# Joint layer norms: the mean subtracted in the application, epsilon added on GpSimd

## The chip, the cores and the metric

The kernel runs on one NeuronCore of a Trainium2 chip. A core has five engines that run side by side, each through its own list of instructions in order: TensorE (PE, matmuls into PSUM), VectorE (DVE), ScalarE (ACT), GpSimd (POOL) and SyncE (SP, which here only issues transfers). They wait for one another by semaphores. The metric is the device time of one execution in microseconds (us). Before the change three runs took 243.38, 243.4 and 242.79 us, the median 243.38.

## The reference

One transformer block over x of 2048 rows by 512. A vector c gives six rows of 512 (sa, ca, ga, sb, cb, gb) that scale and shift. The first half is attention with a sliding window: 32 heads of width 16, each query seeing the 256 last keys. The second half mixes over rows ("token MLP"): two products with w1 (2048 x 1792) and w2 (1792 x 2048) along the row axis. There are three layer norms: of x ahead of the attention, of the sum behind it, and a third at the start of the mixer.

```python
def _layernorm(x, axis=-1, eps=1e-05):
    m = jnp.mean(x, axis=axis, keepdims=True)
    v = jnp.var(x, axis=axis, keepdims=True)
    return (x - m) / jnp.sqrt(v + eps)
...
h = _layernorm(x, axis=-1) * (1 + ca) + sa
x = x + ga * _A_ref(h, A_wqkv, A_wo)          # attention
h = _layernorm(x, axis=-1) * (1 + cb) + sb
x = x + gb * _B_ref(h, B_w1, B_b1, B_w2, B_b2)  # third norm of h, then u = gelu(h^T w1 + b1), y = u w2 + b2
```

## The kernel before

**Tiling.** x lies in 16 blocks of 128 rows (`xres`, named x). Four blocks make a group. Per group the first norm gives xn, which TensorE transposes to h1T (L1142, evacuated by VectorE at L1155 with the scale and shift on the way). From h1T come K, Q and V by matmuls with wqkv (L606 in whole columns, L610 in four column tiles; both are the helper `dense_step`), which VectorE or ScalarE copy out of PSUM (L740, L738: KT, QR, V). Q is padded to QP with a parity mask (L1048). Score matmuls (L819, L837, L847) with mask matmuls (L828, L859) fill a PSUM tile pss of 128 x 1024, of which there are three; ScalarE turns each into et by one exponential (L868), 152 in all. TensorE multiplies et by V (L890) into one of two single banks bk; VectorE transposes the product (t, L899), takes reciprocals (zr, L908), GpSimd merges (L912), VectorE transposes again (OT, L921). The output product with Wo is added to x (L1255).

**Norms.** A norm of one block runs: statistics and their aggregation on VectorE (L599, L600), giving mean and variance in mv; `prepare`, two steps on VectorE, variance plus epsilon (ve, L571) and minus the mean (ng, L575); `rstd`, two steps on GpSimd, ve to the power -1/2 (r, L582) and ng times r (sh, L584); and per block `apply`, x times r plus sh (L592 on VectorE or GpSimd, L588 on ScalarE). Blocks may be normed jointly: their statistics lie side by side, and the four steps between are done once for two or four blocks. The first norms of groups 1 to 3 (n1) are joint over four blocks. Behind the attention, n2 and n3 are joint over 4, 2, 4, 1 and 4, 2, 2, 1 blocks in groups 0 to 3, so the last group norms each block for itself. That makes twelve joint norms (three n1, four n2, five n3) and eight single ones. The first group's own norm, in the opening, has code of its own: the helper `rstd_of` (L553, L555) adds epsilon and takes the power on GpSimd, and L683 subtracts the mean and multiplies on VectorE.

**Second half.** h is scaled by a row (bc_cb) and shifted by a row (bc_sb) at L1273, normed again to hb, and the mixer's first product runs over hb with w1 (L606), in part during the attention, to fill TensorE between the scores. Behind the attention TensorE does what is left of it, ScalarE the gelu, and then the second product with w2 (L1451), whose results VectorE finishes (L1460, L1464) for the store.

**What sets the order.** Everything between the opening and the second product is a task with an engine, an estimated cost, dependencies, a rank from the table `PLACES`, and an engine choice from the table `BY`. The planner `Order` simulates the engines with these costs, picks task after task, and the instructions are emitted in that order; on the chip each engine keeps it. The two steps of `prepare` are one task (`e1`, `e2`, `e3`) of 0.13 us on VectorE, and `rstd` one (`r1`, `q2`, `q3`) on GpSimd. Tiles come from pools that turn over; the small ones (mv, ve, ng, r, sh) four deep for each name.

Of the kernel before, what the change touches and what calls it, by code (L numbers as in the profile page):

```python
# [10 lines left out]
ALU = mybir.AluOpType  # L11
# [336 lines left out]
def kernel(  # L348
# [202 lines left out]
    def rstd_of(var, n, name):  # L551
        ve = small.tile([P, n], DT.float32, name=name + "_ve")
        nc.gpsimd.tensor_scalar(out=ve[:], in0=var, scalar1=EPS, scalar2=0.0, op0=ALU.add, op1=ALU.add)  # L553
        r = small.tile([P, n], DT.float32, name=name)
        nc.gpsimd.tensor_tensor(out=r[:], in0=ve[:], in1=mhalf[:, 0:n], op=ALU.pow)  # L555
        return r

    class Norm:
# [8 lines left out]

        def prepare(self):
            n = self.n
            self.ve = small.tile([P, n], DT.float32, name=self.name + "ve")  # L570
            nc.vector.tensor_scalar(  # L571
                out=self.ve[:], in0=self.mv[:, :, 1], scalar1=EPS, scalar2=0.0, op0=ALU.add, op1=ALU.add
            )
            self.neg = small.tile([P, n], DT.float32, name=self.name + "ng")
            nc.vector.tensor_scalar(  # L575
                out=self.neg[:], in0=self.mv[:, :, 0], scalar1=-1.0, scalar2=0.0, op0=ALU.mult, op1=ALU.add
            )

        def rstd(self):
            n = self.n  # L580
            self.r = small.tile([P, n], DT.float32, name=self.name + "r")
            nc.gpsimd.tensor_tensor(out=self.r[:], in0=self.ve[:], in1=mhalf[:, 0:n], op=ALU.pow)  # L582
            self.shift = small.tile([P, n], DT.float32, name=self.name + "sh")
            nc.gpsimd.tensor_tensor(out=self.shift[:], in0=self.neg[:], in1=self.r[:], op=ALU.mult)  # L584

        def apply(self, eng, i, out, src):
            if eng == "ACT":
                nc.scalar.activation(  # L588
                    out=out, in_=src, func=ACT.Identity, bias=self.shift[:, i : i + 1], scale=self.r[:, i : i + 1]
                )  # L590
            else:
                (nc.vector if eng == "DVE" else nc.gpsimd).tensor_scalar(  # L592
                    out=out, in0=src, scalar1=self.r[:, i : i + 1], scalar2=self.shift[:, i : i + 1],
                    op0=ALU.mult, op1=ALU.add,
                )
# [906 lines left out]
```

## Time and profile before

| | |
|---|---|
| median of three runs | 243.38 us |
| the profiled execution | 242.64 us, of which its span 240.9 us |
| busy: TensorE, VectorE, ScalarE, GpSimd | 234.5, 177.3, 162.1, 96.1 us |
| granted TensorE clock | 1.00 throughout |
| instructions of VectorE, GpSimd | 421, 149 |

How to read it: a row of a timeline has the start in us from the span's start, the duration in us, engine, line, operation and the tiles it writes and reads (output <- inputs), how many neighbours were merged, and in brackets the engine's idle time before it with the instruction that ended that. [...] A row of the waits has who waited for whom, the sum in us, how many times, and the longest. A row of stretches has from and to, the length, and then busy us of each engine with its instructions in brackets, the clock, the share of the DMA engines and GB/s; of one line alone, only the engines that have it.

### The profile page before, as it was taken

Reading aid. Unit: us, or ns where it says so; the run is one execution under the profiler, and the core shown is the slowest. Engines: PE = TensorE matmul, PEld = TensorE weight load, DVE = VectorE, ACT = ScalarE, POOL = GpSimd, SP = SyncE. Lnnn points to the kernel's source line nnn. Section 1 sums busy time; section 2 is a strip of 40 time slices with the busy share of each in tenths; the row PEclk is TensorE's granted clock in tenths of the full one; section 3 lists DMA queues with packets and bytes.
Section 4 is the critical chain, followed back from the end, with each engine's and each line's share of the span. In section 5 each row is a group of like instructions: output and inputs, shape, how many; then the busy total and the mean of one; then the engine's idle time right before and its main releaser. Section 6 shows DMA issues by size and latency. Waiting matters only on the chain.

```text
span 240.9 us, 9884 instructions
## 1 busy us (share of the span) xinstructions
PE 234.5 (97%) x4358; PEld 118.7 (49%) x4358; DVE 177.3 (74%) x421; ACT 162.1 (67%) x188; POOL 96.1 (40%) x149
## 2 busy tenths in 40 slices
PE   7999999999999999999999999999999999999994
PEld 2545555545655554554454455454444444444443
DVE  8799998878999899999356867989964306060644
ACT  7589999999999999999999999900446400000000
POOL 5319775741655466996310113686920000000000
PEclk9999999999999999999999999999999999999999
DMA  5998714063160343210110110069999001111031
GB/s 161 303 345 245 224 32 123 21 169 68 58 181 5 74 113 91 64 35 7 33 38 14 26 38 3 3 199 393 413 405 407 18 0 46 44 44 44 24 111 44
DMA packets 26151, 28.09 MB, mean 117 GB/s; under 512 B 10488, under 2 KB 23292, under 8 KB 26108
## 3 DMA queue, kind: packets, MB, share of 16 engines
q1 hardware_dynamic: 25956, 27.33, 36.0%
q8 instruction: 34, 0.56, 1.0%
q10 hardware_dynamic: 152, 0.13, 0.2%
q14 instruction: 9, 0.07, 0.1%
HBM read 22.55 MB, written 2.10 MB: 102 GB/s over the span
## 4 chain that ended last, share of the span: by engine, by line
PE 74%; DVE 19%; POOL 2%; issue 2%; ACT 2%; DVEq 0%; ACTq 0%; POOLq 0%
PE bk L606 18%; PE pss L1451 15%; PE bk L890 7%; PE pss L606 6%; PE bk L610 6%; PE pss L847 6%; DVE stats L599 5%; PE bk L1451 5%; PE bk L624 3%; DVE x L1255 2%; DVE t L899 2%; PE pss L859 2%; PE pss L819 2%; PE pss L828 1%; DVE QR L740 1%
## 5 line engine op out<-in xcount | busy, mean ns | idle before, releaser
L868 ACT ACTIVATE et<-pss 128x1024 bf16<-128x1024 f32 x152 | 141.7, 1050 | 1.5 <-PE pss L859 1.3
L1451 PEld LDWEIGHTS <-w2r 128*128 128x128 bf16 x238 | 23.1, 98 | 25.5
L912 POOL TENSOR_TENSOR merge<-t,zr 128x512 bf16<-128x512 f32 x16 | 16.9, 1058 | 32.3 <-DVE zr L908 32.2
L1460 DVE SCALAR_TENSOR_TENSOR o<-pss,bFM,bc_gb 128x512 bf16<-128x512 f32 (+2 forms) x13 | 8.8, 705 | 27.9 <-PE pss L1451 27.9
L1451 PE MATMUL pss<-guT,w2r 128*128 128x512 bf16 (+2 forms) x130 | 28.4, 363 | 0.0
L899 DVE STREAM_TRANSPOSE t<-bk 128x512 f32<-128x512 f32 x32 | 22.6, 706 | 7.2 <-PE bk L890 7.0
L847 PE MATMUL pss<-QP,KT 32*128 32x64 bf16 (+2 forms) x672 | 24.2, 236 | 0.7 <-DVE QP L727 0.3
L606 PE MATMUL bk<-h1T,wqkv 128*128 128x512 bf16 x80 | 21.0, 381 | 0.0
L1048 POOL TENSOR_SCALAR QP<-QR,mask_par 128x512 bf16<-128x512 bf16 x22 | 15.1, 694 | 14.8 <-PE pss L859 9.7
L606 PE MATMUL bk<-hb,w1a 128*128 128x512 bf16 x82 | 20.6, 380 | 0.2 <-DVE t L899 0.2
L606 PE MATMUL pss<-hb,w1b 128*128 128x512 bf16 x80 | 20.1, 379 | 0.1
L847 PEld LDWEIGHTS <-KT 32*128 32x128 bf16 x672 | 11.2, 92 | 17.7 <-issue 15.1
L890 PE MATMUL bk<-et,V 128*32 128x256 bf16 (+2 forms) x704 | 19.0, 240 | 0.7 <-DVE t L899 0.4
L599 DVE BATCH_NORM_STATS2 stats<-x 128x6 f32<-128x512 bf16 x28 | 18.8, 673 | 0.2
L890 PEld LDWEIGHTS <-V 128*32 128x32 bf16 x704 | 15.2, 97 | 7.2 <-issue 2.7
L606 PEld LDWEIGHTS <-w1b 128*128 128x128 bf16 x112 | 10.9, 98 | 13.7 <-issue 0.5
L859 PE MATMUL pss<-mask_q,mask_k 32*128 32x256 bf16 x240 | 17.5, 268 | 0.0
L606 PE MATMUL bk<-wod,OT 128*128 128x512 bf16 x54 | 13.9, 381 | 0.0
L606 PEld LDWEIGHTS <-w1a 128*128 128x128 bf16 x90 | 7.9, 98 | 10.3 <-issue 2.5
L606 PE MATMUL bk<-wqkv,h1T 128*128 128x512 bf16 x47 | 12.8, 381 | 0.0
L1255 DVE TENSOR_TENSOR x<-bk,x 128x512 bf16<-128x512 f32 x16 | 10.8, 674 | 2.8 <-PE bk L606 2.8
L921 DVE STREAM_TRANSPOSE OT<-merge 128x512 bf16<-128x512 bf16 x16 | 11.2, 700 | 2.0 <-POOL merge L912 1.8
(145 smaller groups left out, 396.5 us busy)
## 6 DMA issues: line engine op xcount, KB each, us to landing
w2r<-in_B_w_dram SPq DMA_DIRECT2D x14, 512.0 KB, 10.6
w1a<-in_B_w_dram SPq DMA_DIRECT2D x16, 224.0 KB, 3.7
w1b<-in_B_w_dram SPq DMA_DIRECT2D x8, 448.0 KB, 6.7
wmod<-in_w_mod_dram SPq DMA_DIRECT2D x4, 512.0 KB, 6.9
x<-in_A_x_dram SPq DMA_DIRECT2D x15, 128.0 KB, 5.4
out_dram<-otile SPq DMA_DIRECT2D x15, 128.0 KB, 1.8
VL<-V SPq DMA_DIRECT2D x15, 96.0 KB, 2.3
wmod<-in_w_mod_dram SPq DMA_DIRECT2D x4, 256.0 KB, 4.3
```

Of the source, the lines that this page charges most:

```text
L599: nc.vector.bn_stats(out=stats[:], in_=src)
L606: nc.tensor.matmul(out[:], lhsT=lhsT, rhs=rhs, start=start, stop=stop, skip_group_check=True)
L610: nc.tensor.matmul(out[cols, :], lhsT=lhsT[:, cols], rhs=rhs, start=start, stop=stop, tile_position=(0, 32 * j), skip_group_check=True,)
L847: mm(pss[j // 2][:, j % 2, c0 : c0 + nq], lhsT=keys(4 * tg + kb)[rows[j], :], rhs=QP[s][rows[j], par, q0 : q0 + nq], start=n == 0, stop=False,
L859: mm(o, lhsT=mask_k[rows[j], 0:P], rhs=rhs, start=False, stop=True, tile_position=(32 * j, 0), skip_group_check=True,)
L868: nc.scalar.activation(out=et[:], in_=held.pop(("pss", u, a))[:], func=ACT.Exp, scale=SCORE_SCALE)
L890: nc.tensor.matmul(po[32 * j : 32 * j + 32, q0 : q0 + nq], lhsT=v(j), rhs=held["et", s, k, j // 2][:, j % 2, c0 : c0 + nq], start=n == 0, ...
L899: nc.vector.transpose(out=held["t2", s][:, par, :], in_=psum.pop(("po", s, par))[:])
L912: nc.gpsimd.tensor_tensor(out=m[:].rearrange("p (b a d) -> p a b d", a=2, d=DH), in0=t2v(s, 0, DH, DH), in1=held["zr", s][:].to_broadcast( ...
L1048: engine[by(f"Qp{s}.{par}", "POOL")].tensor_scalar(out=QP[s][:, par, :], in0=QR[s][:], scalar1=mask_par[:, par : par + 1], scalar2=0.0, op ...
L1255: nc.vector.tensor_tensor(out=xres[tb][:], in0=pa[:], in1=xres[tb][:], op=ALU.add)
L1451: nc.tensor.matmul(py[:, lo:hi], lhsT=w2r[:, fc, tb * P : (tb + 1) * P], rhs=guT[fc][:, lo:hi], start=fc == made[0], stop=fc == made[-1], ...
```

## The change

For a norm of more than one block, `prepare` emits nothing. `rstd` calls `rstd_of`, so GpSimd adds epsilon to the variance itself and then takes the power; the product of mean and r is not formed. `apply` subtracts the mean and multiplies by r, where it multiplied by r and added a shift. Single norms are as before; they alone are applied on ScalarE, which needs the shift.

```diff
         def prepare(self):
             n = self.n
+            if n > 1:
+                return
             self.ve = small.tile([P, n], DT.float32, name=self.name + "ve")
...
         def rstd(self):
             n = self.n
+            if n > 1:
+                self.r = rstd_of(self.mv[:, :, 1], n, self.name + "r")
+                return
             self.r = small.tile([P, n], DT.float32, name=self.name + "r")
...
+            elif self.n > 1:
+                (nc.vector if eng == "DVE" else nc.gpsimd).tensor_scalar(
+                    out=out, in0=src, scalar1=self.mv[:, i, 0:1], scalar2=self.r[:, i : i + 1],
+                    op0=ALU.subtract, op1=ALU.mult,
+                )
             else:
```

The helper it calls is there already:

```python
    def rstd_of(var, n, name):
        ve = small.tile([P, n], DT.float32, name=name + "_ve")
        nc.gpsimd.tensor_scalar(out=ve[:], in0=var, scalar1=EPS, scalar2=0.0, op0=ALU.add, op1=ALU.add)
        r = small.tile([P, n], DT.float32, name=name)
        nc.gpsimd.tensor_tensor(out=r[:], in0=ve[:], in1=mhalf[:, 0:n], op=ALU.pow)
        return r
```

The planner's costs are not touched, so its order of tasks is the same. The lists of TensorE, ScalarE and SyncE are unchanged; VectorE's has 24 instructions fewer, GpSimd's as many as before. In the changed kernel line numbers from the diff on are higher by up to 10. In the rows below the number behind a tile's name tells buffers apart, and brackets name whom an instruction waits for.

VectorE, before, where the transposes of the second group are evacuated to h1T (28 us in the profile):

```order
L740 CAST QR<-bk_846 128x512 [waits PE_49]
L1155 TENSOR_SCALAR h1T<-bk_862,modFM_93 128x512 [waits PE_49]
L1155 TENSOR_SCALAR h1T<-bk_862,modFM_93 128x512
L571 TENSOR_SCALAR n1ve<-n1mv 128x4 [waits DVE_49]
L575 TENSOR_SCALAR n1ng<-n1mv 128x4
L1155 TENSOR_SCALAR h1T<-bk_900,modFM_94 128x512 [waits PE_49]
L1155 TENSOR_SCALAR h1T<-bk_900,modFM_94 128x512
```

VectorE, after, at the same place:

```order
L750 CAST QR<-bk_842 128x512 [waits PE_49]
L1165 TENSOR_SCALAR h1T<-bk_858,modFM_93 128x512 [waits PE_49]
L1165 TENSOR_SCALAR h1T<-bk_858,modFM_93 128x512
L1165 TENSOR_SCALAR h1T<-bk_896,modFM_94 128x512 [waits PE_49]
L1165 TENSOR_SCALAR h1T<-bk_896,modFM_94 128x512
```

The two pairs of evacuations, which had the third group's two small steps between them, now follow each other.

GpSimd, before, from the application of block 5's second norm on (103 us in the profile):

```order
L592 TENSOR_SCALAR h_3663<-x_69,n2r,n2sh 128x512
L582 TENSOR_TENSOR n3r<-n3ve,mhalf 128x2 [waits DVE_49]
L584 TENSOR_TENSOR n3sh<-n3ng,n3r 128x2 [waits DVE_49,Pool_49]
L1273 TENSOR_TENSOR h_3663<-h_3663,bc_cb_99 128x512
L592 TENSOR_SCALAR hb_116<-h_3408,n3r,n3sh 128x512 [waits Pool_49]
L1273 TENSOR_TENSOR h_3663<-h_3663,bc_sb 128x512 [waits Pool_49]
```

GpSimd, after, at the same place:

```order
L597 TENSOR_SCALAR h_3635<-x_69,n2mv,n2r 128x512
L553 TENSOR_SCALAR n3r_ve<-n3mv 128x2 [waits DVE_49]
L555 TENSOR_TENSOR n3r<-n3r_ve,mhalf 128x2 [waits Pool_49]
L1283 TENSOR_TENSOR h_3635<-h_3635,bc_cb_99 128x512
L597 TENSOR_SCALAR hb_116<-h_3384,n3mv,n3r 128x512 [waits Pool_49]
L1283 TENSOR_TENSOR h_3635<-h_3635,bc_sb 128x512 [waits Pool_49]
```

The addition of epsilon now stands ahead of the power, where the product stood behind it; the wait for VectorE is now for the statistics themselves, and everything else keeps its place.

VectorE, before, where those results are taken up (108 us):

```order
L599 BN_STATS stats<-h_3663 128x6 [waits Pool_49]
L600 BN_AGGR n3mv<-stats 128x2 [waits DVE_49]
L571 TENSOR_SCALAR n3ve<-n3mv 128x2 [waits DVE_49]
L575 TENSOR_SCALAR n3ng<-n3mv 128x2
L899 STREAM_TRANSPOSE t_3884<-bk_3787 128x512 [waits PE_49,Pool_49]
L592 TENSOR_SCALAR hb_117<-h_3399,n3r,n3sh 128x512
```

VectorE, after:

```order
L609 BN_STATS stats<-h_3635 128x6 [waits Pool_49]
L610 BN_AGGR n3mv<-stats 128x2 [waits DVE_49]
L909 STREAM_TRANSPOSE t_3848<-bk_3755 128x512 [waits PE_49,Pool_49]
L597 TENSOR_SCALAR hb_117<-h_3375,n3mv,n3r 128x512
```

The transpose t, which frees a bank for TensorE, now follows the aggregation directly.

## The prediction

> **What bounds the kernel now.** I read the page's busy shares first, then the stretches, then the waits of TensorE, then the timelines of single engines. The page and the table of stretches (us, then busy time of PE, PEld, DVE, ACT, POOL) say:
>
> ```profile
> PE 234.5 (97%) x4358; PEld 118.7 (49%) x4358; DVE 177.3 (74%) x421; ACT 162.1 (67%) x188; POOL 96.1 (40%) x149
> ...
> 13.00:33.00 20.00, 19.34 (x432) 10.16 (x429) 19.58 (x48) 19.55 (x24) 12.83 (x19) 1.00 0.75 232
> 33.00:110.00 77.00, 76.41 (x2124) 41.00 (x2124) 71.12 (x153) 76.93 (x85) 47.89 (x59) 1.00 0.31 80
> 110.00:123.00 13.00, 12.75 (x374) 6.71 (x374) 7.73 (x16) 12.96 (x15) 4.35 (x7) 1.00 0.10 20
> 123.00:157.00 34.00, 33.84 (x904) 17.63 (x906) 26.15 (x57) 33.49 (x36) 9.88 (x12) 1.00 0.10 21
> 157.00:190.00 33.00, 32.94 (x208) 14.99 (x197) 24.19 (x66) 10.40 (x15) 15.29 (x28) 1.00 0.87 334
> ```
>
> From 13 to 157 us two engines are full at once, TensorE with matmuls and ScalarE with the exponentials; from 157 on it is TensorE alone. The chip is not throttled (the clock column is 1.00). VectorE, whose 24 small steps go, is nearly full too up to 110 us, but a VectorE step is worth time only where TensorE or ScalarE waits for it. The waits of TensorE say where:
>
> ```profile
> PE bk L890 <- DVE t L899: 0.4, 1, 0.4
> PE bk L610 <- DVE h1T L1155: 0.3, 1, 0.3
> ...
> PEld L819 <- ACT et L868: 2.5, 6, 0.4
> ```
>
> The last row is ScalarE's hold on TensorE (a score matmul waits until an exponential has emptied its PSUM). It returns all through the attention, so a TensorE gain is given back at the next such wait unless ScalarE moves too. ScalarE's own rhythm:
>
> ```profile
> 25.86 5.77 ACT L868 ACTIVATE et<-pss 128x1024 bf16<-128x1024 f32 x6
> ...
> 32.03 68.60 ACT L868 ACTIVATE et<-pss 128x1024 bf16<-128x1024 f32 x74 [0.40 <-PE pss L859]
> ...
> 110.58 6.90 ACT L868 ACTIVATE et<-pss 128x1024 bf16<-128x1024 f32 x7
> ...
> 32.03 1.02 ACT L868 ACTIVATE et<-pss 128x1024 bf16<-128x1024 f32 x1 [0.40 <-PE pss L859]
> ```
>
> One takes 1.02, and 74 in a row start (68.60 - 1.02) / 73 = 0.926 apart. Twice the rhythm breaks. The sixth of the first row starts at 25.86 + 5.77 - 1.02 = 30.61, the next at 32.03: 1.42 apart, 0.50 lost. From 110.58 seven stand (6.90 - 1.02) / 6 = 0.98 apart: 6 x 0.054 = 0.32 lost. These are the two places that the change can reach, since each lies right behind one of the two TensorE waits on VectorE above.
>
> **The change, part by part.** Removed: in the twelve joint norms, all before 162 us, the additions of epsilon (L571) and the negations of the mean (L575) on VectorE.
>
> ```profile
> 0.00:162.00 162.00, 2.98 (x12) 1.00 0.36 98
> ...
> 0.00:162.00 162.00, 2.79 (x12) 1.00 0.36 98
> ```
>
> That is 2.98 + 2.79 = 5.77 us of VectorE in 24 instructions. Where no long GpSimd instruction is in the way a pair costs 0.14 from start to start (below, 109.34 to 109.48); four steps took far longer, and three of them stand in the chain that ended last. If every piece counted, this would be the gain; two places count.
>
> First place, the evacuation of the second group's transposes; the second row of GpSimd is what n1ng meets:
>
> ```profile
> 27.43 0.98 DVE L1155 TENSOR_SCALAR h1T<-bk,modFM 128x512 bf16<-128x512 bf16 x2
> 28.34 0.16 DVE L571 TENSOR_SCALAR n1ve<-n1mv 128x4 f32<-128x4 f32 x1
> 28.41 0.60 DVE L575 TENSOR_SCALAR n1ng<-n1mv 128x4 f32<-128x4 f32 x1
> 28.91 0.98 DVE L1155 TENSOR_SCALAR h1T<-bk,modFM 128x512 bf16<-128x512 bf16 x2
> ...
> 27.62 1.36 POOL L1048 TENSOR_SCALAR QP<-QR,mask_par 128x512 bf16<-128x512 bf16 x2 [0.46 <-DVE QR L740]
> ...
> 29.95 1.05 PE L610 MATMUL bk<-wqkv,h1T 128*32 128x512 bf16 x16 [0.35 <-DVE h1T L1155]
> ```
>
> n1ng ends at 29.01, when GpSimd's QP pair does (28.98): it stood still behind QP. Without the two steps the second pair of h1T starts 0.57 earlier (28.34 for 28.91). TensorE's 0.35 is then covered, and VectorE's earlier removed pair (0.14, same group of work, VectorE full) can add to it, so the matmuls come 0.35 to 0.49 earlier, and with them the mask matmul for which ScalarE sat idle at 32.03. ScalarE could take up to 0.50. I take 0.45. ScalarE keeps its rhythm behind that, so the gain reaches 110 us.
>
> Second place, the evacuation that TensorE awaits at 110.25, with GpSimd's work ahead of it:
>
> ```profile
> 98.63 0.87 POOL L582 TENSOR_TENSOR n2r<-n2ve,mhalf 128x2 f32<-128x2 f32 x1 [0.35 <-DVE n2ng L575]
> ...
> 103.42 0.77 POOL L592 TENSOR_SCALAR h<-x,n2r,n2sh 128x512 bf16<-128x512 bf16 x1
> 104.29 0.81 POOL L582 TENSOR_TENSOR n3r<-n3ve,mhalf 128x2 f32<-128x2 f32 x1
> 105.18 0.20 POOL L584 TENSOR_TENSOR n3sh<-n3ng,n3r 128x2 f32<-128x2 f32 x1
> ...
> 107.20 1.16 POOL L1273 TENSOR_TENSOR h<-h,bc_sb 128x512 bf16<-128x512 bf16 x1
> ...
> 108.39 0.69 DVE L599 BATCH_NORM_STATS2 stats<-h 128x6 f32<-128x512 bf16 x1 [0.15 <-POOL h L1273]
> ...
> 109.34 0.17 DVE L571 TENSOR_SCALAR n3ve<-n3mv 128x2 f32<-128x2 f32 x1
> ...
> 109.48 0.71 DVE L899 STREAM_TRANSPOSE t<-bk 128x512 f32<-128x512 f32 x1
> ...
> 110.25 0.63 PE L890 MATMUL bk<-et,V 128*32 128x256 bf16 x24 [0.35 <-DVE t L899]
> ```
>
> VectorE's own part: ve and ng right ahead of the transpose, 0.14. The other 0.21 of TensorE's 0.35 must come from GpSimd, since the statistics at 108.39 wait for its addition at 107.20, and whatever VectorE saves before that ends in this wait.
>
> Added on GpSimd: an addition of epsilon in each joint norm, where the product n..sh (L584) goes.
>
> ```profile
> L553 POOL TENSOR_SCALAR r_ve<-mv x2: 242/270/298, 4.9 to 6.7; 128x2 f32<-128x2 f32 x2
> ```
>
> 0.20 goes (105.18 above), 0.27 comes by the same line in the kernel's opening (0.24 to 0.30, for two blocks; I take it for four as well): 12 x 0.07 = 0.84 us more on GpSimd in all, hidden wherever GpSimd waits anyway. At 98.28 it sits idle for 0.35 until n2ng is done; the addition needs only the mean and variance, so it lies in that idle time, the power starts at 98.63 as before, and 0.28 (product and its gap of 0.08) is gained. At 104.19 GpSimd is busy up to then: addition and gap 0.35, product and gap 0.28 less, and the 0.10 before the power gone: 0.03 gained. Together 0.31, more than the 0.21 needed. So this wait goes too; ScalarE's 0.32 is the price. The bounds are 0.12 (ve and ng alone) and 0.32; I take 0.32. Behind 110 TensorE meets ScalarE again, as two score groups of the same form show, the second stretched by such a wait; so nothing above 0.32 passes. The last row is the wait at 151.6, behind both places:
>
> ```profile
> 112.89 0.43 PE L819 MATMUL pss<-QP,KT 32*64 32x128 bf16 x32
> ...
> 122.00 0.55 PE L819 MATMUL pss<-QP,KT 32*64 32x128 bf16 x32
> ...
> 151.63 0.59 PE L606 MATMUL bk<-hb,w1a 128*128 128x512 bf16 x2 [0.16 <-DVE t L899]
> ```
>
> The application changes its operations, not its count: 13 on VectorE, 23 on GpSimd.
>
> ```profile
> 0.00:162.00 162.00, 5.06 (x13) 16.96 (x23) 1.00 0.36 98
> ...
> L683 DVE TENSOR_SCALAR xn<-x,mv,r x4: 378/399/800, 6.5 to 8.5; 128x512 bf16<-128x512 bf16 x4
> ```
>
> On VectorE subtract and multiply is what L683 does already: 0.40 against 5.06 / 13 = 0.39, cost nothing. On GpSimd no row shows that pair of operations; it now takes 16.96 / 23 = 0.74. The low bound is QP's 0.68 (1.36 / 2), the high one the 1.16 of a two-tensor instruction; I take 0.74, as the form and the bytes stay. What the mean must wait for is no later than before, since the statistics precede r. The buffers of mean and variance are held up to the last application instead of the second step; they turn over four deep, and the fifth norm of a kind comes long after the first one's last application, so no wait comes of it. No DMA is touched, and no row of TensorE, ScalarE or SyncE.
>
> In the 33 us behind 157 TensorE has 32.94 of work, so the joint norm that is still open there has nobody waiting. The transpose awaited at 151.6 is the end of a run of VectorE work without a removed step in it, and that wait stays. The sum is 0.45 + 0.32 = 0.77, about 0.8 us. Against the profiled execution (242.64, its span 240.9 and 1.7 around it) that gives 241.8. The median of the three runs, 243.38, lies 0.74 above the profiled one, and the forecast against it is 243.38 - 0.8 = 242.6.
>
> **The rivals.** *The stall is handed on.* QP kept GpSimd busy up to 28.98 and a VectorE step behind it; if the next VectorE instruction stood still as long, nothing would be gained there, and likewise at 103.7: 243.3. Against it speaks that the first pair of h1T ran its 0.98 from 27.43 under the same QP, exactly as the second pair did later. [...]
>
> *Only the first place pays.* If the addition costs GpSimd more than the idle time covers, 0.45 + 0.12 remain: 242.8.
>
> *The whole chain pays.* The chain that ended last runs through VectorE for long, and holds
>
> ```profile
> 28.50 0.51 DVE n1ng L575
> ...
> 86.64 0.70 DVE n3ve L571
> ...
> 103.73 0.48 DVE n3ve L571
> ```
>
> 1.7 us in three steps: 241.7. Against it: TensorE had 76.41 of 77 us busy between 33 and 110, so 1 us is not there to be had; the chain shows one path, not how near the next is.
>
> *Slower: GpSimd's subtract and multiply costs like two-tensor work.* Five applications lie between 96.7 and 108.4:
>
> ```profile
> 96.70:108.40 11.70, 0.00 (x0) 3.84 (x5) 1.00 0.15 40
> ```
>
> At 1.16 each, 0.39 more than 3.84 / 5 = 0.77, the addition at 107.20 comes 2.0 later, less 0.3; TensorE at 110.25 waits 1.7 more, and ScalarE starves behind it. With 0.45 kept that is 1.2 slower: 244.6. It decides from (0.45 + 0.3) / 5 = 0.15 us per application on. For it: nothing in the trace prices that pair on GpSimd. Against it: VectorE takes the same time for both pairs, and the bytes moved are the same.
>
> **How the numbers follow.** 0.3% of 243.38 is 0.73 us, about what a measurement of this kernel can tell from no change. Forecast 0.62, with a range of its own from 242.2 to 243.0; its centre lies just past the bound, and as the early 0.14 and ScalarE's 0.50 lie above what I took, I put two thirds of it (0.41) beyond. The whole chain 0.09; first place only 0.10; handed on 0.06; slower 0.12, and 0.01 for what I don't see. Faster 0.41 + 0.09 = 0.50, same 0.21 + 0.10 + 0.06 = 0.37, slower 0.13. The range 241.7 to 243.6 leaves out the slower case and half of the whole-chain one, 0.17.
>
> **What would show it.** In the changed kernel's profile VectorE has 24 instructions fewer and some 5.5 us less busy time; the wait of L610 on h1T near 29.5 is gone and ScalarE's idle 0.40 near 31.5 is under 0.1; the wait of L890 on t near 109.5 is gone, and seven exponentials there take 6.6; GpSimd's application stays at 0.74 and its new addition at 0.27. An application above 0.9, or a TensorE wait on GpSimd or VectorE of over 0.5 anywhere between 30 and 157 us, would make the forecast wrong; so would ScalarE as slow as now with the two waits gone.

## The result, and the profile after

The changed kernel takes 261.86 us (median of six runs, 260.81 to 263.41) beside 242.83 us for the kernel before in the same comparison: a ratio of 1.0783, 95% interval 1.0740 to 1.0826. It is 19 us slower; 242.6 was forecast. The profiled execution's span is 258.7 us, 17.8 more than before.

The page of the changed kernel, busy times and the granted clock in 40 slices:

```profile
PE 234.2 (91%) x4316; PEld 120.1 (46%) x4358; DVE 174.9 (68%) x397; ACT 162.6 (63%) x188; POOL 126.7 (49%) x149
...
PEclk9999997999999999959999999999999999999999
```

TensorE and ScalarE are busy as long as before (the trace lacks the records of 42 matmuls), VectorE 2.4 us less, in 24 instructions fewer. GpSimd has 30.6 us more in the same 149 instructions. The answer on the application's line L597 (count, then ns least/median/most, first and last start) has all of it:

```profile
L597 POOL TENSOR_SCALAR hb<-h,n3mv,n3r x10: 2068/2078/2082, 94.8 to 180.2; 128x512 bf16<-128x512 bf16 x10
L597 POOL TENSOR_SCALAR xn<-x,n1mv,n1r x8: 2062/2072/2082, 20.8 to 68.3; 128x512 bf16<-128x512 bf16 x8
L597 DVE TENSOR_SCALAR h<-x,n2mv,n2r x7: 401/408/481, 73.7 to 168.7; 128x512 bf16<-128x512 bf16 x7
...
L597 POOL TENSOR_SCALAR h<-x,n2mv,n2r x5: 2066/2082/2342, 105.8 to 161.0; 128x512 bf16<-128x512 bf16 x5
```

On GpSimd an application takes 2.08 us where it took 0.74 to 0.77; on VectorE 0.40 as before. 23 of them make 23 x 1.3 = 30 us more of GpSimd. What that costs shows in TensorE's waits and in ScalarE's exponentials:

```profile
PE bk L616 <- DVE t L909: 5.4, 2, 5.2
PE bk L620 <- DVE V L750: 4.3, 1, 4.3
PE bk L900 <- DVE t L909: 2.1, 1, 2.1
PE pss L616 <- ACT hb L593: 1.5, 1, 1.5
```

```profile
26.54 13.23 ACT L878 ACTIVATE et<-pss 128x1024 bf16<-128x1024 f32 x14
45.39 63.17 ACT L878 ACTIVATE et<-pss 128x1024 bf16<-128x1024 f32 x68 [5.62 <-PE pss L869]
114.39 1.94 ACT L878 ACTIVATE et<-pss 128x1024 bf16<-128x1024 f32 x2 [5.83 <-PE pss L869]
117.72 7.44 ACT L878 ACTIVATE et<-pss 128x1024 bf16<-128x1024 f32 x8 [1.39 <-PE pss L838]
126.82 44.92 ACT L878 ACTIVATE et<-pss 128x1024 bf16<-128x1024 f32 x48 [1.66 <-PE pss L869]
```

The longest wait of TensorE in the attention that names GpSimd is 0.8 us, yet the longer ones in the rows above lead back to it. The timelines of GpSimd, VectorE and TensorE at the first stop:

```profile
32.60 6.19 POOL L597 TENSOR_SCALAR xn<-x,n1mv,n1r 128x512 bf16<-128x512 bf16 x3
...
39.42 1.06 POOL L922 TENSOR_TENSOR merge<-t,zr 128x512 bf16<-128x512 f32 x1
...
40.51 0.71 DVE L931 STREAM_TRANSPOSE OT<-merge 128x512 bf16<-128x512 bf16 x1 [4.62 <-POOL merge L922]
41.15 0.65 DVE L750 CAST V<-bk 128x512 bf16<-128x512 f32 x1
...
41.85 1.26 PE L620 MATMUL bk<-h1T,wqkv 128*32 128x512 bf16 x9 [4.28 <-DVE V L750]
```

Three applications hold GpSimd from 32.60 to 38.79. The merge of an attention unit stands behind them in GpSimd's queue, the transpose OT waits for the merge, the evacuation of V stands behind that transpose in VectorE's queue, and TensorE waits for V's bank, the PSUM tile bk that V is evacuated from. From 92 us on it is the same with other names; GpSimd runs without a gap to 129:

```profile
94.84 6.19 POOL L597 TENSOR_SCALAR hb<-h,n3mv,n3r 128x512 bf16<-128x512 bf16 x3
...
105.79 4.41 POOL L597 TENSOR_SCALAR h<-x,n2mv,n2r 128x512 bf16<-128x512 bf16 x2
...
110.24 0.42 DVE L1283 TENSOR_TENSOR h<-h,bc_cb 128x512 bf16<-128x512 bf16 x1 [1.90 <-POOL h L597]
...
110.91 0.71 DVE L909 STREAM_TRANSPOSE t<-bk 128x512 f32<-128x512 f32 x1
...
111.68 0.58 PE L616 MATMUL bk<-wqkv,h1T 128*128 128x512 bf16 x1 [5.25 <-DVE t L909]
```

The 152 exponentials are a ruler along the whole attention. The table has the start of the exponential of that number (counted from 0; in brackets its time in the kernel before), measured from the first one, less the same in the kernel before, in us: a positive value is time lost so far. The last column is the end of the span, measured likewise. wod is the weight of the output product; e9 to f3 move its transfer, as told below. All values are worked out from the starts in one profiled execution of each kernel.

| kernel | 12 (25.9 us) | 16 (29.7) | 18 (32.0) | 32 (44.8) | 90 (98.7) | 106 (113.6) | end |
|---|---|---|---|---|---|---|---|
| changed kernel | 0.92 | 0.93 | 0.53 | 6.34 | 6.33 | 15.40 | 18.01 |
| steps left out (e4) | 0.06 | 0.07 | -0.01 | -0.01 | 0.00 | -0.25 | -0.25 |
| pair alone (e2) | 0.78 | 0.79 | 3.48 | 4.86 | 4.85 | 15.33 | 18.05 |
| quick pair (e1) | 0.00 | -0.08 | 0.29 | 0.29 | 0.29 | 0.04 | 0.22 |
| slow pair in norms of four blocks (e5) | 1.18 | 1.20 | 0.73 | 7.47 | 7.47 | 10.16 | 10.16 |
| slow pair in norms of two blocks (e6) | 0.37 | 0.38 | -0.03 | -0.02 | -0.01 | 6.97 | 9.61 |
| repaired (e7) | 0.36 | 0.37 | 1.12 | 1.13 | 1.14 | 1.24 | 1.25 |
| steps left out, wod at 34 us (e9) | 0.34 | 0.35 | -0.06 | 0.12 | 0.14 | -0.11 | -0.10 |
| before, wod at 34 us (e10) | 0.17 | 0.19 | 0.19 | 0.62 | 0.62 | 0.61 | 0.60 |
| repaired, wod at 34 us (e11) | 0.37 | 0.38 | -0.04 | 0.74 | 0.85 | 0.95 | 0.95 |
| one step for two, wod at 34 us (e12) | 0.04 | 0.06 | -0.35 | 0.15 | 0.15 | 0.22 | 0.74 |
| before, wod at 27 us (f0) | 0.83 | 0.85 | 0.84 | 0.84 | 0.85 | 0.83 | 0.82 |
| steps left out, wod at 27 us (f1) | 0.30 | 0.31 | -0.10 | -0.10 | -0.02 | -0.27 | -0.26 |
| repaired, wod at 27 us (f2) | 0.35 | 0.37 | -0.05 | -0.05 | -0.06 | 0.05 | 0.06 |
| one step for two, wod at 27 us (f3) | 0.00 | -0.04 | -0.46 | -0.46 | -0.41 | -0.34 | 0.06 |

The changed kernel loses 0.9 up to number 12, 5.8 between 18 and 32 (the first stop), 9.1 between 90 and 106 (the second), and 2.6 behind the attention.

### The profile page after: what moved, and what is told of

Same layout as the page of the kernel before. It is cut to its first block, busy times and chain, and to the rows that moved or that the text cites. A ratio compares the mean times of both kernels' runs of the same rounds, so it can differ in the third digit from the quotient of the medians.

```text
span 258.7 us, 9807 instructions
## 1 busy us (share of the span) xinstructions
PE 234.2 (91%) x4316; PEld 120.1 (46%) x4358; DVE 174.9 (68%) x397; ACT 162.6 (63%) x188; POOL 126.7 (49%) x149
## 4 chain that ended last, share of the span: by engine, by line
PE 56%; POOL 25%; issue 4%; DMA 4%; DVE 4%; SPq 3%; ACT 2%; POOLq 0%; ACTq 0%
PE pss L1461 14%; PE bk L616 14%; POOL hb L597 7%; PE bk L900 5%; PE pss L857 5%; PE pss L616 5%; PE bk L1461 5%; PE bk L620 5%; POOL h L597 3%; POOL xn L597 3%; POOL merge L922 3%; POOL h L1283 3%; DMA x<-in_A_x_dram 2%; DMA wmod<-in_w_mod_dram 2%; POOL QP L1058 2%
## 5 line engine op out<-in xcount | busy, mean ns | idle before, releaser
L922 POOL TENSOR_TENSOR merge<-t,zr 128x512 bf16<-128x512 f32 x16 | 16.9, 1056 | 30.6 <-DVE zr L918 30.6
L900 PE MATMUL bk<-et,V 128*32 128x256 bf16 (+2 forms) x704 | 19.8, 246 | 2.2 <-DVE t L909 2.1
L597 POOL TENSOR_SCALAR hb<-h,n3mv,n3r 128x512 bf16<-128x512 bf16 x10 | 20.7, 2077 | 0.3
L616 PE MATMUL bk<-hb,w1a 128*128 128x512 bf16 x76 | 19.9, 380 | 0.8 <-issue 0.5
L616 PE MATMUL bk<-h1T,wqkv 128*128 128x512 bf16 x67 | 18.8, 381 | 0.7 <-issue 0.3
L597 POOL TENSOR_SCALAR xn<-x,n1mv,n1r 128x512 bf16<-128x512 bf16 x8 | 16.5, 2072 | 1.2 <-PE bk L1152 1.0
L620 PE MATMUL bk<-h1T,wqkv 128*32 128x512 bf16 x160 | 11.7, 401 | 4.3 <-DVE V L750 4.3
```

The source lines that it names most:

```text
L597: (nc.vector if eng == "DVE" else nc.gpsimd).tensor_scalar(out=out, in0=src, scalar1=self.mv[:, i, 0:1], scalar2=self.r[:, i : i + 1], op0 ...
L616: nc.tensor.matmul(out[:], lhsT=lhsT, rhs=rhs, start=start, stop=stop, skip_group_check=True)
L620: nc.tensor.matmul(out[cols, :], lhsT=lhsT[:, cols], rhs=rhs, start=start, stop=stop, tile_position=(0, 32 * j), skip_group_check=True,)
L900: nc.tensor.matmul(po[32 * j : 32 * j + 32, q0 : q0 + nq], lhsT=v(j), rhs=held["et", s, k, j // 2][:, j % 2, c0 : c0 + nq], start=n == 0, ...
L922: nc.gpsimd.tensor_tensor(out=m[:].rearrange("p (b a d) -> p a b d", a=2, d=DH), in0=t2v(s, 0, DH, DH), in1=held["zr", s][:].to_broadcast( ...
```

## The experiments

The theory after the result was that the pair of operations is dear on GpSimd, whatever its operands. The rivals: the scalar taken from the statistics tile is dear, or the moved small steps are.

### The changed kernel with another pair of operations (e1)

```diff
+            elif self.n > 1:   # on GpSimd
+                nc.gpsimd.tensor_scalar(
+                    out=out, in0=src, scalar1=self.r[:, i : i + 1], scalar2=self.mv[:, i, 0:1],
+                    op0=ALU.mult, op1=ALU.add,
+                )
```

> The changed kernel, but GpSimd's joint applications multiply by r and add the mean (the sign and the scale of the shift are left out, so the result differs from the reference); tiles read, small steps and VectorE's applications are as in the changed kernel. Theory A (GpSimd is slow for the pair subtract, multiply): its 23 applications fall from 2.07 back to 0.77 us, and the time to what was forecast for the whole change, about 0.8 us under before (242.0 against 242.8). Theory B (it is slow because a scalar is read out of mv, two values per block, written by VectorE): they stay at 2.07 and the time at 261 to 262. Theory C (the added epsilon step and the moved waits on GpSimd cost the time, the slow application only fills what is idle): 0.77 each, yet the time stays over 250.

243.37 us, ratio 1.0004 (0.9983 to 1.0025). Its page, the application's group (busy us, mean ns):

```profile
L602 POOL TENSOR_SCALAR hb<-h,n3r,n3mv 128x512 bf16<-128x512 bf16 x10 | 7.7, 773 | 0.3
```

Same tiles, same statistics tile as a scalar, the small steps moved, and 0.77 us an application. Both rivals fall. But the forecast's 0.8 us does not appear either.

### The application alone (e2)

```diff
+            elif self.n > 1:   # the kernel before; prepare and rstd as they were
+                (nc.vector if eng == "DVE" else nc.gpsimd).tensor_scalar(
+                    out=out, in0=src, scalar1=self.mv[:, i, 0:1], scalar2=self.r[:, i : i + 1],
+                    op0=ALU.subtract, op1=ALU.mult,
+                )
```

> The kernel before with one part of the change: joint applications subtract the mean and multiply by r. VectorE's two small steps and GpSimd's power and product stay (the product is then read by nobody in joint norms). Theories A and B: 2.07 us an application on GpSimd and a time about as the changed kernel's plus the 0.8 us that its left-out steps were to save, 262 to 264. Theory C: within 1 us of before.

260.29 us, ratio 1.0715 (1.0682 to 1.0748), applications of 2.08. The pair alone brings the slowdown, with the small steps where they were. The time lies below the expected 262 to 264: beside stops of this size the small steps can't be priced (the profiled executions end 18.05 and 18.01 behind the kernel before).

### Eight pairs in one kernel (e3)

GpSimd's joint applications take eight pairs in turn, on lines 597 to 611; the first two are shown.

```diff
+                r, s = self.r[:, i : i + 1], self.shift[:, i : i + 1]
+                if nth[0] % 8 == 0:
+                    nc.gpsimd.tensor_scalar(out=out, in0=src, scalar1=r, scalar2=s, op0=ALU.mult, op1=ALU.add)
+                elif nth[0] % 8 == 1:
+                    nc.gpsimd.tensor_scalar(out=out, in0=src, scalar1=s, scalar2=r, op0=ALU.subtract, op1=ALU.mult)
...
```

> The kernel before, in which GpSimd's 23 joint applications take eight pairs of operations in turn, each on a source line of its own, all with the scalars r and shift of before (so the normed values are wrong in most blocks). Theory A: multiply, add takes 0.77 and subtract, multiply 2.07 with these scalars too; which of the other six are slow tells whether it is the subtraction, a multiplication in second place, or everything but multiply, add. If only the subtraction: four of eight slow. If only multiply, add is fast: seven slow. Theory B: all eight at 0.77.

251.18 us in its one run. The groups (mult, add; add, mult; mult, mult; then subtract, mult; mult, subtract; subtract, add; add, add; subtract, subtract):

```profile
L597 POOL TENSOR_SCALAR hb<-h,n3r,n3sh 128x512 bf16<-128x512 bf16 x2 | 1.5, 770 | 0.1
...
L601 POOL TENSOR_SCALAR hb<-h,n3sh,n3r 128x512 bf16<-128x512 bf16 x1 | 0.8, 773 | 0.0
...
L609 POOL TENSOR_SCALAR hb<-h,n3r,n3sh 128x512 bf16<-128x512 bf16 x1 | 0.8, 776 | 0.0
...
L599 POOL TENSOR_SCALAR hb<-h,n3sh,n3r 128x512 bf16<-128x512 bf16 x2 | 4.2, 2078 | 0.1
...
L603 POOL TENSOR_SCALAR hb<-h,n3r,n3sh 128x512 bf16<-128x512 bf16 x2 | 4.2, 2084 | 0.0
...
L605 POOL TENSOR_SCALAR hb<-h,n3sh 128x512 bf16<-128x512 bf16 x1 | 2.1, 2091 | 0.0
...
L607 POOL TENSOR_SCALAR hb<-h,n3sh 128x512 bf16<-128x512 bf16 x1 | 2.1, 2090 | 0.1
...
L611 POOL TENSOR_SCALAR xn<-x,n1sh 128x512 bf16<-128x512 bf16 x1 | 2.1, 2084 | 0.0
```

There are two prices and nothing between: 0.77 for three pairs, 2.08 to 2.09 for all with a subtraction and for two additions. So it is not subtraction as such; which other pairs are quick was not tried.

### The two steps left out, nothing else (e4)

```diff
+            if n > 1:
+                self.ve, self.neg = self.mv[:, :, 1], self.mv[:, :, 0]
+                return
```

> The kernel before, in which joint norms leave out VectorE's two small steps and nothing is added: GpSimd takes the power of the variance and multiplies by the mean straight out of mv (epsilon and the sign of the shift are left out of the result); applications multiply and add as before. This measures the forecast's gain alone. The forecast: the wait of L610 on h1T near 29.5 us and that of L890 on t near 110 are gone, ScalarE's idle 0.40 near 32 is under 0.1, and the time is 0.8 us below before (0.4 to 1.2). Rival (stalls are handed on, or hidden by ScalarE's rhythm): within 0.3 us of before.

243.54 us, ratio 1.0016 (0.9994 to 1.0037): the gain of the forecast without its cost is not there. In the table the second place is: 0.25 gained between 90 and 106 (0.32 was forecast). The first is not, though L610's wait on h1T is gone. TensorE's timeline has another hold in its place:

```profile
30.25 0.81 PE L893 MATMUL bk<-et,V 128*32 128x256 bf16 x15
30.84 0.23 PE L893 MATMUL bk<-et,VL 128*32 128x64 bf16 x6
```

In the kernel before 16 of these take 0.50; here nothing starts between 30.47 and 30.80. In e1 the same hold lasts from 30.31 to 31.09, with "issue" as its cause: no engine is waited for.

### The slow pair in norms of four blocks, then of two (e5, e6)

The changed kernel; in e5 the slow pair stays for n == 4, in e6 for n == 2, and the other GpSimd applications are those of e1.

```diff
-            elif self.n > 1:
+            elif self.n > 1 and (eng == "DVE" or self.n == 4):
```

> The changed kernel, but only the 8 GpSimd applications of the norms of four blocks (n1) subtract and multiply; the 15 of the norms of two blocks on GpSimd multiply by r and add the mean (so the sign and the product with r are left out of those rows). Theory A, each stall has its own place and the places add: of the changed kernel's lost time the exponentials lose 5.6 us behind the n1 applications at 32.6 to 38.8 us, and that stays: 249 us (247 to 251), n1 applications 2.07 us, the other GpSimd applications 0.77, the wait of L620 on V over 3 us, none over 1 us behind 100 us. Theory B, GpSimd is short of time as a whole and the first stall is only where it shows first: 23 slow applications made 19 us, 8 of them make little until GpSimd is full, under 245.

> The changed kernel with the roles turned round: the 15 GpSimd applications of the norms of two blocks (n2, n3) subtract and multiply, the 8 of the norms of four blocks multiply by r and add the mean (sign and product left out there). Theory A (places add): the exponentials behind 100 us lose 5.8, 1.4 and 1.7 us and the end 2.7, 11.6 in all: 254.5 us (252 to 257), no wait over 1 us between 30 and 90 us, and with the run that keeps the n1 applications slow the two excesses add to 17 to 20 us. Theory B (GpSimd full as a whole): most of the 19 us stays with 15 of the 23, over 257, or the two excesses add to far less than 19.

253.05 us (ratio 1.0385, 1.0353 to 1.0418) and 253.14 us (1.0407, 1.0368 to 1.0446). The excesses add: 9.6 and 9.7 us, 19.4 together, beside 19.0 for the whole change. So the losses add, as the first theory has it. But the edit does not part n1 from n2 and n3, as the expectations say: n2 and n3 are joint over four blocks in some groups. On GpSimd 13 applications are slow in e5 (eight of n1, four of n3, one of n2) and 10 in e6, where the forecast shares (249 and 254.5) were for 8 and 15. The four of n3, and what waits behind them, in e5:

```profile
L597 POOL TENSOR_SCALAR hb<-h,n3mv,n3r x4: 2068/2074/2079, 96.2 to 103.1; 128x512 bf16<-128x512 bf16 x4
...
108.01 0.43 DVE L1288 TENSOR_TENSOR h<-h,bc_cb 128x512 bf16<-128x512 bf16 x1 [2.04 <-POOL h L602]
...
110.48 0.81 PE L621 MATMUL bk<-wqkv,h1T 128*128 128x512 bf16 x3 [2.64 <-DVE t L914]
```

So e5's loss up to number 32 is n1's, and its 2.7 between 90 and 106 lie behind the four of n3. n1's last slow application ends at 71.72, and GpSimd's idle times between 75 and 94 are nearly as long as in the kernel before (9.3 us in sum beside 9.9). ScalarE in e5, then in e6:

```profile
46.11 1.94 ACT L883 ACTIVATE et<-pss 128x1024 bf16<-128x1024 f32 x2 [5.87 <-PE pss L874]
...
112.04 9.51 ACT L883 ACTIVATE et<-pss 128x1024 bf16<-128x1024 f32 x10 [2.06 <-PE pss L874]
```

```profile
117.89 1.94 ACT L883 ACTIVATE et<-pss 128x1024 bf16<-128x1024 f32 x2 [4.08 <-PE pss L874]
```

### The change repaired (e7)

```diff
+                self.r = rstd_of(self.mv[:, :, 1], n, self.name + "r")
+                self.neg = small.tile([P, n], DT.float32, name=self.name + "ng")
+                nc.gpsimd.tensor_scalar(
+                    out=self.neg[:], in0=self.mv[:, :, 0], scalar1=-1.0, scalar2=0.0, op0=ALU.mult, op1=ALU.add
+                )
...
+                nc.gpsimd.tensor_scalar(
+                    out=out, in0=src, scalar1=self.neg[:, i : i + 1], scalar2=self.r[:, i : i + 1],
+                    op0=ALU.add, op1=ALU.mult,
+                )
```

> The change with a quick pair: VectorE's two small steps stay out, GpSimd adds epsilon, takes the power and negates the mean, and its application adds the negated mean and multiplies by r (0.77 in the run that tried pairs); VectorE's applications subtract and multiply. Everything is computed. Theory I, TensorE's code caps the first place: two runs with the steps out showed TensorE standing still inside the attention matmuls at 30.47 to 30.80 and at 30.31 to 31.10 us with no wait on any engine, 1.46 and 1.53 us behind the end of a 16,384-byte transfer on the instruction queue (29.34 and 29.57); the kernel before, whose transfer ended at 29.42, reaches that matmul only at 31.04. So here too: a stop at the same matmul, ScalarE idle 0.3 to 0.7 near 31.8, gain in the first place 0 to 0.1, in the second 0 to 0.25, and 243.1 us (242.6 to 243.4) beside a kernel before of 243.1. Theory G, the added GpSimd steps (epsilon and negation 0.27 each for one product of 0.20) are paid at the second place: L900's wait on t near 110 is back at 0.3 or more, 243.4. Theory F, the forecast's sum holds with quick applications: 242.4.

243.73 us, ratio 1.0016 (0.9997 to 1.0035). Applications of 0.77, and the hold at the same matmul, longer than ever:

```profile
30.54 0.47 PE L909 MATMUL bk<-et,V 128*32 128x256 bf16 x11
31.92 0.26 PE L909 MATMUL bk<-et,V 128*32 128x192 bf16 x4 [0.91 <-issue]
```

The second place loses 0.1 instead of gaining 0.25, as theory G had it: two GpSimd steps for one.

What TensorE waits for stands in the records of the DMA queues. The page of the kernel before has a queue of kind "instruction":

```profile
q8 instruction: 34, 0.56, 1.0%
```

34 transfers of 16,384 bytes beside TensorE's 8716 matmuls and weight loads: if they bring TensorE's instructions, its code, about 256 come with each (8716 / 34), and e8 below bears that out. The place where one transfer's instructions end and the next one's begin is called a border here. The holds lie at the same number in TensorE's list, whatever the time (from the trace's records; start of the last instruction ahead and of the first one behind). The traces of the kernel before, e10 and e11 have all 8716 records; the others of the table lack some, so that the same border has a number lower by 3 to 5 there:

```
kernel   number  code transfer    TensorE         restart behind its end
before    958    28.47 to 29.42   no hold, 31.04        1.62
e4        954    28.12 to 29.34   30.47 to 30.80        1.46
e1        954    28.63 to 29.57   30.31 to 31.09        1.52
e7        954    29.33 to 30.52   30.77 to 31.92        1.40
e8        953    27.15 to 28.09   28.66 to 29.73        1.64
e7        699    22.73 to 23.98   24.87 to 25.45        1.46
f2        699    23.02 to 23.96   24.89 to 25.44        1.48
e10      1469    37.17 to 38.20   39.24 to 39.64        1.44
e11      1469    37.08 to 38.42   39.00 to 39.74        1.32
```

The distance is kept beyond the holds too: in the five traces with all 8716 records none of the 30 borders from number 702 to 8126, 256 apart, is crossed sooner than 1.28 us behind the end of its transfer (in the kernel before none sooner than 1.52, at 702). The kernel before crosses the one at 31.04 only 1.62 behind, so bringing TensorE there earlier is worth at most 0.34 us (1.62 - 1.28, an estimate) as long as the code lands when it does. The transfer for this border starts 3.2 us after the border before it is crossed (25.27 in the kernel before), while the DMA engines move 326 GB/s (25.2 to 28.4 us).

### The border moved (e8)

```diff
-        warm(11)
+        warm(94, 16)
```

> The repaired change, and in the opening 94 idle matmuls of 16 columns for 11 of 512: about the same time, 83 matmuls with their weight loads more, so that the border between two 16,384-byte pieces of TensorE's code (34 pieces for 8716 matmuls and weight loads, so 256 instructions each) falls 45 matmuls later, behind the attention matmuls of 31 us instead of inside them. Theory I (code caps the first place): no stop inside the attention matmuls at 30 to 31.2, ScalarE idle under 0.1 near 31.5 where the repaired change has 0.3 to 0.7; if the opening is as long, 242.7 us, 0.3 to 0.5 below the repaired change. Rival, the stop has another cause (the data of the attention matmuls, or the DMA traffic itself): the stop of 0.3 to 0.8 stays at the same matmul, time as the repaired change. Second rival, the border meets the traffic at another place: the stop is gone there, and another of 0.3 or more with no wait on an engine stands elsewhere before 33 us.

245.33 us, ratio 1.0073 (1.0048 to 1.0099). The second rival came true: the attention matmuls run through, and a hold of 1.08 stands 83 matmuls ahead of the old place, in front of a group of transposes, at number 953 (and one of 0.41 at number 698). The border itself had stayed at its number, and other work had moved into it. That the hold kept its number while other work stood there is the best evidence for the code. The time is longer because the opening is: the first exponential starts at 14.12, 1.3 later than in e7, with eight transposes of L707 at 1.06 us where they take 0.72 behind the long idle matmuls; the clock records show full speed from 11.73 us on, in e7 from 5.23.

### The traffic ahead of the code moved (e9 to e12, f0 to f3)

To the kernels above one change is added, in SyncE's list: the 512 KB of wod, issued at 22.4 us, go behind the third copy of V's edges (about 34 us, as shown), or behind the second bias row (about 27 us). e12 and f3 are the kernel before with, besides that, VectorE's two steps in one instruction, in the single norms too.

```diff
-        later("wo", wod[:], wo_v, 512, 12)
...
             dma.dma_start(out=VU[s % 2][64:128, 2:4, :, :], in_=Vring[tg % 3][64:128, 0:2, hs, :])
+            if copied[0] == 3:
+                dma.dma_start(out=wod[:], in_=wo_v)
```

```diff
+            both = small.tile([P, n, 2], DT.float32, name=self.name + "ve")
+            nc.vector.scalar_tensor_tensor(
+                out=both[:], in0=self.mv[:], scalar=EPS, in1=signs[:, 0:n, :], op0=ALU.add, op1=ALU.mult
+            )
```

> The run with VectorE's two steps left out (no epsilon, sign of the mean not turned, nothing else changed on GpSimd), and one transfer moved: the 512 KB of wod are issued behind the third copy of V's edges (about 34 us) instead of at 22.4 us. No engine but SyncE has another order. So far the stop stood at the 957th matmul or weight load of TensorE in three kernels, also where 83 matmuls more stood ahead of it, 1.40 to 1.65 us behind the end of a 16,384-byte code transfer, and that transfer started about 3 us after TensorE crossed the border before it (700th at 25.2 us, start at 28.1), while the 16 DMA engines were full. Theory I (TensorE waits for code that is late behind data): without wod's 1.5 us of traffic the transfer starts 1 us or more earlier, no stop at that matmul, ScalarE idle under 0.1 near 31.4, the forecast's 0.45 in the first place appears and the 0.23 of the second stays: 242.5 us (242.2 to 242.8) beside 243.2 before. Rival T (the stop is not the code, or wod is not what delays it): a stop of 0.3 or more stays in the attention matmuls near 30.5, 243.2 to 243.5.

> The kernel before with wod's transfer moved in the same way, nothing else. Theory I: there the matmul at the border starts at 31.04, and the code was there by about 30.9, so earlier code is worth 0.1 at most; L610's wait of 0.35 on h1T and ScalarE's idle 0.40 at 32.03 stay: 243.1 us (within 0.3 of the kernel before). Rival T: moving wod is a gain of its own (lighter traffic in the opening), 0.4 or more: 242.7, and then what the other runs of this batch gain is not the change's.

> The repaired change (GpSimd adds epsilon, negates the mean, adds and multiplies; everything is computed) with wod's transfer moved. Theory I: first place gains 0.45, the stop of 1.15 of the repaired run is gone; the second place pays for GpSimd's two more steps (wait on t near 110 was 0.5 there for 0.35 before): 243.0 us (242.7 to 243.2), and over 0.4 below the repaired change. Rival T: as the repaired change, 243.5 or more.

> The kernel before with VectorE's two small steps made in one instruction (mean and variance plus epsilon, times -1 and 1, so that the mean carries an error of 1e-5; everything else is computed as before, GpSimd's steps and applications too), and wod's transfer moved. If the one step does not stand behind GpSimd's QP as n1ng did: first place 0.4, second 0.15, 242.7 us (242.4 to 242.9). Rival: the one step stands still behind QP up to 28.98, L610's wait of 0.3 stays and 243.1 comes out.

At 34 us: 243.19 (ratio 0.9989, 0.9973 to 1.0006), 243.27 (1.0001, 0.9990 to 1.0012), 242.65 (0.9983, 0.9971 to 0.9994) and 243.53 (1.0015, 1.0001 to 1.0029). The hold at this border (954, or 958 of the full list) is gone in all four, and with it ScalarE's idle time at 32 us wherever the steps are out. But the times forecast for e9 (242.5) and e12 (242.7) did not come. e9:

```profile
25.98 130.28 ACT L871 ACTIVATE et<-pss 128x1024 bf16<-128x1024 f32 x140
```

Between numbers 16 and 18 the table has 0.41 or 0.42 gained in e9 and e11, nothing in e10: this is the forecast's first place, 0.45. One step instead of two gains as much there (0.41 in e12, 0.42 in f3) and nothing at the second place. In e9 and e11 the gain only makes good a loss: they are held for 0.56 and 0.57 at the border at 25 us (number 702, 699 in the shorter lists) and stand 0.34 and 0.37 behind at number 12. The gain is also paid back at number 1469: with wod's traffic there, the code for the border at 39 us now comes later (37.17 to 38.20 in e10 and 37.08 to 38.42 in e11, 36.03 to 37.02 in the kernel before), and e10, e11 and e12 lose 0.43, 0.78 and 0.50 between exponentials 18 and 32.

> The kernel before with the 512 KB of wod issued at about 27 us, behind the second bias row, for 22.4 us. Theory I (TensorE's gains are capped by code that is late behind data): nothing to gain here, as this kernel's own waits at 29.95 and 110.25 remain: 243.2 us, within 0.3 of the kernel before. Rival T: the lighter traffic is a gain of its own, 242.8 or less.

> VectorE's two steps left out (no epsilon, sign of the mean not turned, nothing added on GpSimd), wod at about 27 us. Theory I: code on time at the borders of 25, 31 and 39 us, the 18th exponential 0.4 earlier against the first one than in the kernel before and the 106th 0.65, and 242.6 us. Rival T: wod now lies in front of the code for the border at 31 us, which starts at 28.1 or later: a stop of 0.3 or more stays there and the time is 243.2.

> The repaired change (everything computed: epsilon and the mean's sign on GpSimd, application by adding and multiplying), wod at about 27 us. Theory I: 0.4 gained in the first place, 0.1 lost in the second to GpSimd's two more steps, 242.9 us. Rival T: as the repaired change, 243.5 or more.

> VectorE's two steps in one instruction (the mean carries an error of 1e-5), GpSimd as in the kernel before, wod at about 27 us. Theory I: 0.4 gained in the first place, nothing in the second (the run with wod at 34 us showed none there), 242.8 us. Rival T: 243.2 or more, a stop for code of 0.3 or more at one of the borders.

At 27 us: 242.76 (0.9986, 0.9972 to 1.0001), 242.77 (0.9985, 0.9970 to 1.0000), 242.71 (0.9980, 0.9968 to 0.9993) and 243.02 (0.9994, 0.9979 to 1.0010). The borders at 31 and 39 us are on time in all four. In f1 first place and second place both pay, 0.41 and 0.25, and the hold at number 699 (25 us) takes 0.3 of it. In f3, held at 25 us for 0.08 only, 0.46 is gained up to number 18 and 0.34 is left at 106; 0.40 is lost behind the attention, where TensorE waits 0.5 for ScalarE's hb. The timed runs give the move of the transfer alone as much as the move with the steps out: f0 and f1 differ by 0.01 us, and f0 is as quick as its rival T said (242.8 or less). Theory I wanted 0.6 between them, so as a forecast of the time it failed, though the traces show its parts; f0's own hold at 25 us is shorter (0.12) but its profiled execution lost 0.83 up to exponential 12 for reasons that I did not trace, so where the timed difference stays is open. The quickest of all, f2 and e11, lie 0.2% under the kernel before, less than the 0.3% that count here.

## Why the prediction was wrong

**The step that failed** is the price of the application on GpSimd: "The low bound is QP's 0.68 (1.36 / 2), the high one the 1.16 of a two-tensor instruction; I take 0.74, as the form and the bytes stay". It measured 2.08 (e2, e3, and the changed kernel itself), above the upper bound by 0.92. The nearest rows were of other pairs, and neither the bytes nor the number of inputs sets the price: e1 moves the same bytes from the same tiles in 0.77. VectorE's equal time for both pairs (0.40 and 0.39), which I held against a dear one, says nothing about GpSimd; L683 is a row of VectorE only.

**The rival on the slower side** had the mechanism: five applications ahead of the addition at 107.20, TensorE waiting at the transpose t, ScalarE starving. By its own formula 1.31 more for each makes 5 x 1.31 - 0.3 = 6.3 us at the second place; 9.1 came. Four things it lacked. It counted five applications there, and the four of n3 ahead of them (94.84 to 103.76), slow too, stand for 2.7 there in e5. It looked at one place only, and the first stop, 5.8 us behind applications at 32.6 to 38.8, stood where GpSimd had 1.17 idle in the kernel before. It had nothing behind the attention (2.6). And it left out what TensorE's stop does to its clock (below). With 2.08 for its 1.16 it would have said about 249.

**The sum of 0.77** held in its mechanism and not in the time. The wait of L610 on h1T is gone without the steps; four evacuations of h1T follow each other; the first place measures 0.41 of 0.45 where the code is there in time, the second 0.25 of 0.32 with nothing added on GpSimd and -0.1 with two steps added (e7). What I costed at nothing was TensorE's code: "ScalarE keeps its rhythm behind that, so the gain reaches 110 us" is true only where the next border's code is there. The kernel before sits near that edge at two borders (25.27 behind a transfer's end at 23.75, and 31.04 behind 29.42), so TensorE, come earlier, is held there, for 0.3 to 1.15 as the transfer happens to land. VectorE's busy time fell by 3.0 us in e4, not by the 5.5 forecast: neighbours overlap (the two steps of the first place have 0.16 + 0.60, but 0.57 from start to start), so a line's own sum is more than what leaves with it.

**Right were** the price of the added epsilon (0.27 forecast; in e1 the medians of the three kinds of norm are 0.23 to 0.24), VectorE's application (0.40), the second removed wait (e4), the rival *handed on*, which did not occur (h1T ran its four evacuations in 1.89 under QP in e4), and the signs by which the forecast said it would fail: an application above 0.9, and a wait of TensorE on VectorE above 0.5.

## What to carry to other kernels

Price an instruction on GpSimd by its operations as well as its shape: for 128x512 bf16 with two scalars, (mult, add), (add, mult) and (mult, mult) cost 0.77 us here, the five other pairs tried 2.08. Write a subtraction as the addition of a negated scalar there (0.77 in e7). And where a few tenths are to be won in a stretch of dense small matmuls under heavy loading, look up when TensorE's next 256 instructions land: if they land 1.3 to 1.6 us before they are needed, as at the borders of the table above, little is to be won ahead of that point.

## What the runs showed of the hardware that was not expected

The two long stops of TensorE in the changed kernel cost more than their length. Stretches of the changed kernel (busy us of PE, PEld, DVE, ACT and POOL, then the granted clock), where TensorE started no matmul from 37.31 to 41.85:

```profile
40.00:42.00 2.00, 0.15 (x4) 0.12 (x7) 1.49 (x3) 0.00 (x0) 1.92 (x4) 1.00 0.79 244
42.00:44.00 2.00, 2.00 (x33) 1.18 (x29) 1.09 (x3) 0.00 (x0) 0.47 (x1) 0.52 0.11 40
44.00:46.00 2.00, 2.00 (x59) 1.50 (x50) 1.39 (x3) 0.61 (x1) 0.23 (x1) 0.63 0.03 8
46.00:48.00 2.00, 1.95 (x46) 0.93 (x46) 1.93 (x4) 2.00 (x3) 2.00 (x3) 1.00 0.01 4
```

The trace's clock records have half the clock from 42.07 to 45.48, and again from 110.34 to 117.16. By the rows that is 2 x 0.48 + 2 x 0.37 = 1.7 us of TensorE; behind the second stop (clock 0.50, 0.50 and 0.71 from 112 to 118) 2.6 by the same sum. So about 4 of the 18 us are the clock's, an estimate. TensorE's busy time says the like: 234.2 us beside 230.4 in e1, whose trace lacks the same number of records.

The length of a stop alone does not decide. In e5 no matmul starts from 107.57 to 110.48, 2.91 us, and the clock stays (first row); in e2 none starts from 30.39 to 32.63, 2.24 us, and it falls to half at 33.19 (second and third row):

```profile
110.00:112.00 2.00, 1.52 (x30) 0.67 (x33) 1.97 (x5) 0.00 (x0) 2.00 (x4) 1.00 0.00 0
...
32.63 1.40 PE L615 MATMUL bk<-wqkv,h1T 128*32 128x512 bf16 x16 [1.97 <-DVE h1T L1160]
...
33.00:35.00 2.00, 2.00 (x60) 1.31 (x52) 1.65 (x4) 0.00 (x0) 2.00 (x2) 0.55 0.04 12
```

In all 18 traces the clock changes only in steps of whole windows of 3.41 us, counted from its first record (in the changed kernel it stays for 37.55, 3.41, 64.85, 6.83 and 143.36 us: 11, 1, 19, 2 and 42 windows). From full, it fell at the end of every window in which the recorded matmuls left TensorE idle for 0.58 of it or more (0.94 and 1.00 ahead of 42.07 and 110.34 in the changed kernel), and of none with 0.49 or less (e3). e2's stop lies in one window, 29.78 to 33.19, idle for 0.58 of it; e5's is divided by a window's end at 109.03, 0.35 in one and 0.42 in the next. So in these traces a window need not be idle throughout for the clock to fall.

TensorE's code is itself traffic: the transfers of the table take 0.9 to 1.3 us, TensorE goes on 1.3 to 1.6 us behind their end, and the profile calls the hold "issue" (0.91 in e7), or puts it down to another engine (in e8 to an evacuation of h1T, for 0.8; in e11 to the transpose t, for 0.7).
